# GraphSAGE aggregation on one Trainium2 core: output blocks scaled by GpSimd, gather positions added by GpSimd

## The chip, the cores and the metric

The kernel runs on one core of one Trainium2 chip. The metric is device time in microseconds (us), the median of several runs. The engines go by the names of the profile: PE (TensorE matmul) and PEld (its weight loads), DVE (VectorE), ACT (ScalarE), POOL (GpSimd) and SP (SyncE, which here only issues transfers). Each engine works through its own instructions in order; semaphores tie the engines together. SBUF is the core's working memory, PSUM the memory that PE writes its sums to; ACT and DVE read PSUM here, POOL does not.

## The reference

A graph has N = 12500 nodes with D = 64 features each and E = 800000 edges (source, destination). For each node the features of its neighbours are summed, scaled by the inverse of its degree, and two small matrix products are added.

```python
N, deg, D = 12500, 64, 64
E = N * deg
def reference(x, src, dst, deg_inv, w_self, w_neigh):
    N = x.shape[0]
    nsum = _segment_sum(x[src], dst, N)
    h_neigh = nsum * deg_inv[:, None]
    return x @ w_self + h_neigh @ w_neigh
```

The edges are random, so gathering and scattering 800000 rows is the work. `deg_inv` is a factor per destination node; since it scales whole rows, it can be applied before or after the product with `w_neigh`.

## The kernel before, in words

The kernel first sorts and then multiplies. Each edge becomes one 32-bit key made of a destination block (82 x 2 nodes), a source block (128 nodes) and the two places within them. In the first half DVE sorts 128 runs of 6250 keys (`sort_runs`), cuts them at super-rows, gathers the pieces by indirect transfers, and merges them (`merge_runs`). There are three parts, part 0, 1 and 2, with 29, 20 and 10 buckets a row; a bucket is one pair of destination block and source block. Meanwhile `self_terms` writes `x @ w_self` to the output.

In the second half `nodes` walks over 7546 buckets, eight at a time; eight buckets are a tile, and one iteration of the loop is one tile. For each set of 28 buckets DVE builds two sets of one-hot matrices: `ohs` (L935), from the source places that SP has loaded to `slb` (L933), and `ohd` (L940), from the destination places. PE multiplies `ohs` with the table of features into the PSUM tile `ct` (L966); ACT evicts `ct` to `xg` (L976), and late in the kernel DVE does some of these evictions (L974); PE multiplies `xg` with `ohd` into two accumulators `acc` (L1047). Keys that fit in no bucket are fetched one by one by POOL's indirect transfers into `lx` (L997) and added by one more pair of matmuls (L1015).

After six destination blocks (588 buckets, some 74 tiles) the accumulators are copied to `g`, and `finish` makes two output blocks of 4 x 123 nodes from it: PE multiplies with the weights into the PSUM tile `po` (L1114), ACT evicts it to the SBUF tile `o` and scales each of the four sub-blocks by its own column of `self.deg` (L1117), and, five tiles of the loop later, POOL issues the transfer that adds `o` to the output in memory (L1123). There are 26 such blocks; the last has one sub-block of 123 nodes and one of 77. `po` takes one of the three PSUM buffers that `ct` uses.

While part 0 is being multiplied, parts 1 and 2 are still merged by DVE, a little per tile (`PACE`). When a part is merged, `change` finds its buckets: for bucket column k DVE counts how many keys of each row lie below (L708, into column k of `acc`), four columns later ACT adds the base position and writes an unsigned integer (L762, into `ix`), and POOL gathers the window of 128 rows at those positions into `v` (L742). `decode_buckets` then splits the keys (DVE, L782), narrows them (ACT, L791 to L796) and lets POOL store them to `sl` (L794), from which `slb` is loaded. The narrowed tiles `l16` have two buffers, so ACT waits for the stores. Part 1 has 20 columns and part 2 has 10; part 0 goes another way, with DVE doing the positions.

The order on each engine is that of the Python code (`manual_schedule`): `finish`, `change` and the gathers of `lx` are placed by counts of tiles, not by due times. So POOL's queue in the second half holds, in one order, the gathers of `lx` and `v`, the stores of `sl` and of merged rows, and the output's transfers.

Of the kernel before, what the change touches and what calls it, by code (L numbers as in the profile page):

```python
# [17 lines left out]
OP = mybir.AluOpType  # L18
AF = mybir.ActivationFunctionType
# [3 lines left out]
N, E, D = 12500, 800000, 64  # L23
# [350 lines left out]
class Kernel:  # L374
# [371 lines left out]
    def find_and_gather(self, part, vp):  # L746


        nc = self.nc
        kpr = KPRS[part]  # L750
        self.v = vp.tile([128, kpr, 2 * SIDE], I32, name="v")
        acc = self.keep.tile([128, kpr], F32, name=f"acc2_{part}")
        ix = self.keep.tile([128, kpr], U32, name=f"ix2_{part}")
        junk = vp.tile([128, max(n for _, n in WIN.w2[part])], BF, name="junk")
        for k in range(kpr + LAG):
            if k == 1:
                self.store_rows(part, nc.gpsimd)
            if k < kpr:
                self.count_below(part, k, acc, junk)
            if k >= LAG:  # L760
                g = k - LAG
                nc.scalar.activation(ix[:, g:g + 1], acc[:, g:g + 1], AF.Relu, bias=self.c2[part][:, 3, g:g + 1])  # L762
                self.gather_window(part, g, ix)
            yield k

# [339 lines left out]
    def finish(self, qq, g, pool, mps, w, add=False):  # L1105

        nc = self.nc
        if not add:
            own = self.load_own(qq, pool)
        po = mps.tile([FB, 4, D], F32, name="po", tag="ct", bufs=3)  # L1110
        o = pool.tile([FB, 4, D], F32, name="o", bufs=2)
        for b0, nb, n, r in self.sets(qq):
            for b in range(b0, b0 + nb):
                nc.tensor.matmul(po[:n, b], g[:, b * FB:b * FB + n], w[:g.shape[0]], start=True, stop=True)  # L1114
        for b0, nb, n, r in self.sets(qq):
            for b in range(b0, b0 + nb):
                nc.scalar.activation(o[:n, b], po[:n, b], AF.Copy, scale=self.deg[:n, 4 * qq + b:4 * qq + b + 1])  # L1117
        yield
        for b0, nb, n, r in self.sets(qq):
            at = slice(b0, b0 + nb)  # L1120
            out = self.O["out"][r:r + nb * n].rearrange("(b p) f -> p b f", p=n)
            if add:
                nc.gpsimd.dma_start(out, o[:n, at], accum_op=OP.add)  # L1123
            else:
                nc.vector.tensor_tensor(o[:n, at], o[:n, at], own[:n, at], op=OP.add)
                nc.gpsimd.dma_start(out, o[:n, at])
# [286 lines left out]
```

## Time and profile before

| what | value |
|---|---|
| median of 3 runs | 1871.68 us (1863.13 to 1876.03) |
| profiled execution, own time | 1856.37 us |
| its span, first to last instruction | 1854.6 us |
| mean granted clock of PE | 0.775 |
| DVE busy in the span | 1718.2 us (93%) |
| ACT busy in the span | 1116.7 us (60%) |
| PE busy in the span | 986.6 us (53%) |
| POOL busy in the span | 576.2 us (31%) |
| ACT evicting `xg` (L976) | 919 operations, 862.6 us |
| ACT evicting `o` (L1117) | 102 operations, 24.3 us |
| ACT adding positions (L762) | 30 operations, 10.2 us |

A row of a group of instructions reads: line, engine, operation, the tile written <- the tiles read, shape written <- shape read, xcount, then busy us and mean ns of one, then the idle time of the engine just before them and what ended it. A row of the timeline has start, duration (both us), engine, line, operation, and in brackets the idle time before it and its releaser. A row of waits has who waited for whom, then us in total, times, longest us. Busy time is the union of an engine's instructions; neighbours on ACT overlap a little, so a row's mean can be longer than its distance to the next start.

### The profile page before, as it was taken

How to read it: one execution, taken by the hardware profiler on the slowest of the kernel's cores; microseconds unless marked ns; L12 is line 12 of the kernel's file. 1: busy time of each engine (PE TensorE's matmuls, PEld its weight loads, DVE VectorE, ACT ScalarE, POOL GpSimd, SP SyncE). 2: the span in 40 equal slices, each digit the busy share in tenths (PEclk: the TensorE clock that was granted, in tenths of full speed). 3: DMA queues.
4: the chain of work that ended last, by engine and by line, in shares of the span. 5: the costliest groups of instructions: out<-in, count | busy, mean ns of one | idle time of the engine just before them, and what ended most of it. 6: DMA issues, size and time to landing. Idle time of an engine off the chain costs nothing.

```text
span 1854.6 us, 54153 instructions
## 1 busy us (share of the span) xinstructions
PE 986.6 (53%) x23413; PEld 851.9 (46%) x23413; DVE 1718.2 (93%) x1718; ACT 1116.7 (60%) x1587; POOL 576.2 (31%) x447
## 2 busy tenths in 40 slices
PE   3046000000000000058979979897898899888996
PEld 1015000000000000057868868776887788777885
DVE  6999999999999999989989999998898799978885
ACT  5263000113001005458979989899999899977885
POOL 2000000055502005404456535473332523532331
PEclk7567555555555555579989999999999999999998
DMA  5207100021002002169978888996889788977894
GB/s 174 54 0 169 39 0 0 38 79 51 18 4 73 10 0 82 47 216 266 274 249 253 251 248 254 296 282 227 264 250 284 234 265 242 326 200 257 274 268 118
DMA packets 176789, 307.79 MB, mean 166 GB/s; under 512 B 127885, under 2 KB 133596, under 8 KB 175772
## 3 DMA queue, kind: packets, MB, share of 16 engines
q1 hardware_dynamic: 98268, 275.58, 44.9%
q0 software_dynamic: 78272, 28.65, 9.6%
q8 instruction: 185, 3.03, 0.7%
q14 instruction: 64, 0.52, 0.1%
HBM read 277.01 MB, written 26.52 MB: 164 GB/s over the span
## 4 chain that ended last, share of the span: by engine, by line
DVE 19%; PE 13%; DMA 11%; issue 10%; SPq 5%; POOL 4%; ACT 4%; DVEq 0%; POOLq 0%; ACTq 0%
DMA slb<-sl 10%; PE ct L966 7%; DVE u L328 7%; PE acc L1047 5%; SPq L933 5%; DVE ohs L935 4%; DVE ohd L940 3%; ACT xg L976 2%; DVE u L362 2%; POOL u L565 1%; POOL lx L997 1%; POOL out L1123 1%; DVE u L316 1%; DMA sl<-l 1%; PE acc L1015 1%
## 5 line engine op out<-in xcount | busy, mean ns | idle before, releaser
L976 ACT ACTIVATE xg<-ct 128x1024 f16<-128x1024 f32 x919 | 862.6, 1074 | 104.4 <-PE ct L966 80.0
L966 PE MATMUL ct<-xh,ohs 128*128 128x128 f16 x7546 | 532.6, 224 | 87.9 <-DVE ohs L935 23.7
L966 PEld LDWEIGHTS <-ohs 128*128 128x128 f16 x7546 | 451.8, 100 | 125.4 <-issue 52.5
L328 DVE TENSOR_TENSOR u<-u 128x1512 f32<-128x1512 f32 (+57 forms) x316 | 425.7, 1362 | 12.9 <-ACT u L312 8.6
L1047 PE MATMUL acc<-ohd,xg 64*128 64x82 f16 x15092 | 395.2, 201 | 47.7 <-ACT xg L976 20.4
L1047 PEld LDWEIGHTS <-xg 64*128 64x128 f16 x15092 | 324.6, 96 | 104.6 <-issue 29.2
L997 POOL DMA_INDIRECT lx<-xt,ls x127 | 232.0, 1826 | 425.6 <-PE acc L1015 352.5
L940 DVE TENSOR_TENSOR ohd<-iota,dlT 128x2296 f16<-128x2296 bf16 x270 | 362.2, 1341 | 0.0
L935 DVE TENSOR_SCALAR ohs<-slb,pidx 128x3584 f16<-128x3584 bf16 x270 | 321.8, 1192 | 40.2 <-DMA slb<-sl 19.0
L509 PE MATMUL stp<-cx,swapa 128*128 128x16 f32 (+1 forms) x12 | 3.1, 335 | 398.0 <-DVE swapa L505 398.0
L260 DVE TENSOR_TENSOR a<-b 128x1040 f32<-128x1040 f32 (+41 forms) x130 | 194.7, 1539 | 3.5 <-DVE b L260 0.5
L260 DVE TENSOR_TENSOR b<-a 128x1040 f32<-128x1040 f32 (+46 forms) x150 | 194.6, 1345 | 3.2 <-ACT a L262 0.4
L538 POOL DMA_INDIRECT u<-d,ixa x48 | 72.5, 1511 | 390.8 <-ACT junka L526 335.4
L509 PEld LDWEIGHTS stp<-cx,swapa 128*128 128x128 f32 x12 | 2.6, 271 | 398.5 <-DVE swapa L505 398.5
L312 ACT ACTIVATE u<-u 128x256 f32<-128x256 f32 (+14 forms) x60 | 33.0, 618 | 170.6 <-DVE u L316 134.8
L1123 POOL DMA_DIRECT2D out<-o x27 | 99.1, 3800 | 103.1 <-ACT o L1117 89.8
L802 PE MATMUL tr<-idb,l 128*128 128x128 bf16 x59 | 7.6, 263 | 188.9 <-ACT l L796 188.9
L262 ACT ACTIVATE b<-a 128x2 f32<-128x2 f32 (+31 forms) x41 | 15.9, 402 | 127.1 <-DVE a L260 120.4
L802 PEld LDWEIGHTS <-l 128*128 128x128 bf16 x59 | 4.3, 114 | 191.2 <-ACT l L796 190.8
L316 DVE TENSOR_TENSOR u<-u 128x2016 f32<-128x2016 f32 (+11 forms) x40 | 61.9, 1563 | 16.2 <-DMA u<-da,ixb 8.8
L262 ACT ACTIVATE a<-b 128x1 f32<-128x1 f32 (+24 forms) x34 | 8.6, 259 | 105.4 <-DVE b L260 99.9
L565 POOL DMA_INDIRECT u<-da,ixb x24 | 36.9, 1539 | 88.6 <-ACT ixb L513 85.0
(158 smaller groups left out, 839.4 us busy)
## 6 DMA issues: line engine op xcount, KB each, us to landing
slb<-sl SPq DMA_DIRECT2D x1076, 224.0 KB
xt<-xh SPq DMA_DIRECT2D x1, 3136.0 KB
out<-o POOLq DMA_DIRECT2D x25, 123.0 KB
own<-os SPq DMA_DIRECT2D x12, 256.0 KB
out<-os SPq DMA_DIRECT2D x12, 256.0 KB
rd<-dst SPq DMA_DIRECT2D x5, 512.0 KB
rs<-src SPq DMA_DIRECT2D x5, 512.0 KB
lx<-xt,ls POOLq DMA_INDIRECT x127
```

Source lines behind the costliest of these rows:

```text
L260: nc.vector.tensor_tensor(view(dst, lo + sh, [[st, g], [1, l]]), x, y, op=op)
L316: nc.vector.tensor_tensor(at(oth, to, n), x, y, op=op)
L328: nc.vector.tensor_tensor(to, at(cur, ln + lo, n), at(cur, lo + k, n), op=op)
L538: nc.gpsimd.indirect_dma_start(out=u[:, i * w:(i + 1) * w], out_offset=None, in_=src, in_offset=bass.IndirectOffsetOnAxis(ap=self.start[pa ...
L933: nc.sync.dma_start(b[j::4], bass.AP(tensor=src.tensor, offset=src.offset, ap=[[0, 32], [1, n * 128]]))
L935: nc.vector.tensor_scalar(s.rearrange("p c s -> p (c s)"), b, self.pidx[:, :1], None, op0=OP.is_equal)
L940: nc.vector.tensor_tensor(d, self.iota[:, None].to_broadcast(wide), ix, op=OP.is_equal)
L966: nc.tensor.matmul(ct[:, i * 128:(i + 1) * 128], cols[i][0], self.xh[:, (b0 + i) % NB].rearrange("p a f -> p (a f)"), start=True, stop=True)
L976: nc.scalar.activation(xg[:, :cnt * 128], ct[:, :cnt * 128], AF.Copy)
L997: nc.gpsimd.indirect_dma_start(out=x, out_offset=None, in_=self.xt, in_offset=bass.IndirectOffsetOnAxis(ap=self.left[p][1][:, c:c + 1].bit ...
L1047: nc.tensor.matmul(acc[h][:, db % OCT * HN:(db % OCT + 1) * HN], xg[r, i * 128:(i + 1) * 128], d[r], start=db % OCT == 0 and sb == 0, stop ...
L1123: nc.gpsimd.dma_start(out, o[:n, at], accum_op=OP.add)
```

## The change

Two places change. In `finish`, one ACT operation without a factor evicts all sub-blocks of a set from `po` to `o`, and one POOL `tensor_tensor` multiplies `o` in place with the degree factors, each column of `self.deg` broadcast along the 64 features. In the gathers of parts 1 and 2, the addition of the base position moves from ACT (with a Relu) to POOL, on the queue that issues the gather itself.

```diff
@@ -759,7 +759,7 @@
             if k >= LAG:
                 g = k - LAG
-                nc.scalar.activation(ix[:, g:g + 1], acc[:, g:g + 1], AF.Relu, bias=self.c2[part][:, 3, g:g + 1])
+                nc.gpsimd.tensor_scalar(ix[:, g:g + 1], acc[:, g:g + 1], self.c2[part][:, 3, g:g + 1], None, op0=OP.add)
                 self.gather_window(part, g, ix)
             yield k
@@ -1113,8 +1113,10 @@
         for b0, nb, n, r in self.sets(qq):
-            for b in range(b0, b0 + nb):
-                nc.scalar.activation(o[:n, b], po[:n, b], AF.Copy, scale=self.deg[:n, 4 * qq + b:4 * qq + b + 1])
+            at = slice(b0, b0 + nb)
+            nc.scalar.activation(o[:n, at], po[:n, at], AF.Copy)
+            scale = self.deg[:n, 4 * qq + b0:4 * qq + b0 + nb]
+            nc.gpsimd.tensor_tensor(o[:n, at], o[:n, at], scale[:, :, None].to_broadcast([n, nb, D]), op=OP.mult)
         yield
```

## The prediction

> **What bounds the kernel now.** I read the page first. Its busy rows and the strips of 40 slices (46.4 us each) show two halves.
>
> ```profile
> span 1854.6 us, 54153 instructions
> ...
> PE 986.6 (53%) x23413; PEld 851.9 (46%) x23413; DVE 1718.2 (93%) x1718; ACT 1116.7 (60%) x1587; POOL 576.2 (31%) x447
> ...
> DVE  6999999999999999989989999998898799978885
> ACT  5263000113001005458979989899999899977885
> ```
>
> Up to slice 16 (about 790 us) DVE sorts and ACT has little to do; nothing in the change lies there. From slice 18 on, where the sums of the nodes run, DVE and ACT both show 8s and 9s. So I asked for windows of that half (columns: PE, PEld, DVE, ACT, POOL busy, then granted clock, DMA share, GB/s).
>
> ```profile
> 1000.00:1200.00 200.00, 176.20 (x4518) 155.88 (x4513) 197.28 (x203) 181.43 (x218) 94.45 (x40) 0.97 0.87 263
> 1200.00:1300.00 100.00, 86.10 (x2117) 74.41 (x2115) 90.72 (x138) 96.20 (x139) 50.95 (x39) 0.97 0.82 258
> 1300.00:1600.00 300.00, 270.07 (x6851) 239.27 (x6848) 277.69 (x333) 280.78 (x364) 115.47 (x67) 0.97 0.86 262
> ...
> sum 965.00, PE 837.70 PEld 742.75 DVE 873.78 ACT 855.45 POOL 396.04; mean PE 139.62 PEld 123.79 DVE 145.63 ACT 142.57 POOL 66.01
> ```
>
> No single engine bounds this half: DVE leads from 1000 to 1200 us (98.6%), ACT from 1200 to 1300 (96.2%), and the DMA engines stand at 0.82 to 0.87. POOL has room (396 of 965 us). The chain of waits, for 890 to 1845 us, says which of them ends last:
>
> ```profile
> by line: DMA slb<-sl 17.7%; issue 17.3%; PE ct L966 12.0%; PE acc L1047 9.0%; SPq L933 7.6%; DVE ohs L935 7.2%; DVE ohd L940 5.3%; ACT xg L976 4.3%; DVE u L328 3.3%; POOL u L565 2.5%; POOL lx L997 1.7%; POOL out L1123 1.5%; DMA sl<-l 1.0%;
> ```
>
> Two loops carry it. One is DVE (ohs, ohd, u: 15.8%) with the slb loads that a finished ohs sets free (DMA 17.7%, SPq 7.6%): 41.1% together. The other is PE; ACT's evictions are only 4.3%. The table of waits for the same stretch agrees that ACT is as often waiting as waited for:
>
> ```profile
> ACT xg L976 <- PE ct L966: 70.9, 88, 8.0
> ...
> PE ct L966 <- ACT xg L976: 21.1, 23, 3.8
> ...
> PE acc L1047 <- ACT xg L976: 20.4, 15, 4.8
> ```
>
> ACT stood 88 times for PE, once in some 11 us; PE stood 41.5 us for ACT.
>
> **What ACT loses.** The two lines that change, in the groups, and their places in ACT's timeline (start, us, what):
>
> ```profile
> L1117 ACT ACTIVATE o<-po,deg 123x64 f32<-123x64 f32 x102 | 24.3, 351 | 7.5 <-PE po L1114 7.1
> ...
> L762 ACT ACTIVATE ix<-acc,c 128x1 uint32<-128x1 f32 x30 | 10.2, 339 | 0.0
> ...
> 981.01 0.93 ACT L1117 ACTIVATE o<-po,deg 123x64 f32<-123x64 f32 x4
> 981.81 12.93 ACT L976 ACTIVATE xg<-ct 128x1024 f16<-128x1024 f32 x14
> ...
> 1223.72 0.34 ACT L762 ACTIVATE ix<-acc,c 128x1 uint32<-128x1 f32 x1
> 1223.90 1.99 ACT L976 ACTIVATE xg<-ct 128x1024 f16<-128x1024 f32 x2
> ...
> 1836.98 0.38 ACT L976 ACTIVATE xg<-ct 128x256 f16<-128x256 f32 x1 [0.68 <-PE ct L966]
> ```
>
> The mean durations mislead: the next operation starts before the last has ended. From start to start four evictions take 0.80 us and one position 0.18 us. An eviction of 256 columns from PSUM takes 0.38 us by the last row, which I count as 0.28 from start to start (the x4 row overlaps its successor by 0.13 us, so 0.1 is an estimate from it). Of the 102 evictions 100 are 25 whole blocks; the last block keeps its two narrow ones. ACT so loses 25 x (0.80 - 0.28) = 13.0 us and 30 x 0.18 = 5.4 us, 18.4 us in all.
>
> How much of it reaches the end? Bounds: ACT's share of the chain gives 0.043 x 18.4 = 0.8 us, everything gives 18.4. Where ACT leads, 1200 to 1300 us, I count all: by the source lines' own windows there are 14 of the 30 positions and 8 narrow evictions (two blocks) there.
>
> ```profile
> 1200.00:1300.00 100.00, 5.46 (x14) 0.97 0.82 258
> ...
> 1200.00:1300.00 100.00, 2.01 (x8) 0.97 0.82 258
> ```
>
> That is 14 x 0.18 + 2 x 0.52 = 3.6 us. Of the other 14.8 us I count a tenth, 1.5 us, nearer to the chain's 4.3% than to ACT's busy share, since a wait for PE that comes every 11 us swallows a saving of 0.2 to 0.5 us. Term: **-5 us**.
>
> **What POOL gains.** 27 multiplications (25 of 123x256, two of 64 columns) and 30 additions of one column. No row of before has POOL arithmetic on two inputs. The nearest are these:
>
> ```profile
> L396 POOL MEMSET edge<- 128x1 f32 x1 | 0.1, 98 | 0.0
> ...
> masks.py:197 POOL MEMSET idf<- 128x128 f32 x1 | 0.2, 204 | 0.3 <-POOLq L1403 0.3
> ...
> masks.py:199 POOL TENSOR_SCALAR_AFFINE_SELECT idf<-idf 128x128 f32<-128x128 f32 x1 | 0.3, 282 | 0.0
> ...
> masks.py:199 POOL TENSOR_SCALAR_AFFINE_SELECT idb<-idb 128x128 bf16<-128x128 bf16 x1 | 1.2, 1246 | 0.0
> ```
>
> Writing costs 98 ns and 0.83 ns a column; reading one input adds 78 ns over 128 columns, 0.6 ns each. Two inputs over 256 columns: 98 + 256 x (0.83 + 1.2) = 0.62 us, so I take 0.6. The floor is writing alone, 0.31 us; the ceiling is the slow bf16 row taken twice, 2.5 us. An addition I take as 0.2 us (0.1 to 0.3). POOL's own 27 x 0.6 + 30 x 0.2 = 22.2 us fit in its idle time; what counts is whom they hold up.
>
> **DVE** first. POOL and DVE do hold each other up in this trace (a memset of 0.20 us beside the ohs of DVE, then an ohs beside the output's DMA):
>
> ```profile
> 1441.90 0.20 POOL L425 MEMSET pad<- 128x100 f32 x1
> ...
> 1443.87 1.03 POOL L425 MEMSET pad<- 128x100 f32 x1
> ...
> 1443.63 1.16 DVE L935 TENSOR_SCALAR ohs<-slb,pidx 128x3584 f16<-128x3584 bf16 x1 [0.59 <-PE ct L966]
> ...
> 1468.87 4.15 POOL L1123 DMA_DIRECT2D out<-o  x1 [2.87 <-ACT o L1117]
> ...
> 1469.28 2.48 DVE L935 TENSOR_SCALAR ohs<-slb,pidx 128x3584 f16<-128x3584 bf16 x1
> ...
> L940 DVE TENSOR_TENSOR ohd<-iota,dlT 128x2296 f16<-128x2296 bf16 x247 | 331.3, 1341 | 0.0
> L935 DVE TENSOR_SCALAR ohs<-slb,pidx 128x3584 f16<-128x3584 bf16 x246 | 294.1, 1195 | 31.0 <-PE ct L966 18.3 <-DMA slb<-sl 12.0 <-DVE ohd L940 0.2
> L328 DVE TENSOR_TENSOR u<-u 128x736 f32<-128x736 f32 (+43 forms) x160 | 157.5, 995 | 1.8 <-ACT u L312 0.7
> ```
>
> The memset took 1.03 us and ended at 1444.90, just after the ohs (1444.79); the ohs took 2.48 us where its like took 1.16. By what these rows show, ohs is the one that collides: it fills 294.1 of 955 us, 31%, so DVE would lose 0.31 x 22.2 = 6.9 us. The bounds are nothing (POOL always waits) and all of DVE's lines with two inputs besides (331.3 + 294.1 + 157.5 = 782.9 us, 82%): 18.2 us. I weigh it with the 41.1% of DVE's loop in the chain: 2.8 us, nearest to the ohs row, the only one that stretched. Term: **+3 us**.
>
> The Trainium skill (SBUF — State Buffer, "Who interferes with whom") has a rule against this change: DVE and GpSimd share one pair of ports as an exclusive lock, held for the whole instruction, and a DVE instruction with two SBUF inputs collides with a GpSimd one that reads SBUF. For ohs the trace agrees (2.48 against 1.16 us); for the two-input lines no run here shows it, since POOL's rows beside them only write or issue. By that rule the loss would be the 82% bound, 18.2 us, and the term +7.5 in place of +3.
>
> **POOL's queue** next. An addition takes the place of a wait for ACT, but it waits for DVE; a multiplication stands five tiles ahead of its output's DMA and waits for ACT, and the lx, v and sl transfers behind it wait too. Elsewhere POOL idles between two lx; the one full stretch is this (POOL, then ACT):
>
> ```profile
> 1224.33 1.38 POOL L742 DMA_INDIRECT v<-d,ix  x1 [3.82 <-ACT ix L762]
> ...
> 1249.78 1.70 POOL L997 DMA_INDIRECT lx<-xt,ls  x1 [0.30 <-issue]
> 1252.60 0.58 POOL L794 DMA_DIRECT2D sl<-l  x1 [1.12 <-ACT l L792]
> ...
> 1257.99 0.72 ACT L791 ACTIVATE l<-w,edge 128x512 bf16<-128x512 int32 x1 [1.03 <-DMA sl<-l]
> ...
> 1208.16 0.07 DVE L708 DVE_READ_ACCUMULATOR junk<-u,c 128x1 f32 x1
> ```
>
> The gather at 1224.33 (first row) is the thirteenth of part 1; its count was ready on DVE at 1208.2 (last row), so the 3.82 us of waiting for ACT fall away. Behind it stand 8 additions at 0.2 + 0.3 (the gap before a gather) and 2 multiplications at 0.6 + 0.3: 5.8 us. Later by 2.0 us, of which the idle 1.12 before the sl store covers most: **+0.9 us** on ACT, which waits for that store. If each of the ten also waits out a DVE operation, as the memset did (0.83 us), it is +9. If the cover went altogether, the l16 buffers would halt ACT, and PE after it.
>
> **The tail** has nothing beside it:
>
> ```profile
> 1840.68 1.31 ACT L1117 ACTIVATE o<-po,deg 123x64 f32<-123x64 f32 x6 [1.34 <-PE po L1114]
> ...
> 1842.04 5.22 POOL L1123 DMA_DIRECT2D out<-o  x3 [38.41 <-ACT o L1117]
> ```
>
> ACT ends 0.5 us sooner; POOL adds one wide multiplication (0.6) and two narrow (0.2 to 0.3 each): **+0.7 us** (0 to 1.5). PE gets its po buffer back 0.5 us sooner, 25 times; that is inside ACT's term. Order of work on PE, DVE and SP stays.
>
> **Sum.** -5 + 3 + 0.9 + 0.7 = -0.4, about nothing. The profiled execution took 1856.37 us (span 1854.6), 0.8% below the median of 1871.68, so I add the difference to the median: 1871 us.
>
> **The rivals.** *ACT's saving comes through whole.* For it: ACT is over 90% busy in each window from 1000 to 1600 us, and PE stood 41.5 us for it. Against: the 70.9 us it stands for PE. -18.4 + 0.9 + 0.7 = -17: 1855 us. Chance 0.2.
>
> *POOL's multiplications shut DVE out.* The mechanism is the collision above on all two-input lines, from 890 us on, at DVE's busy share of 0.905 (873.78 of 965) instead of 0.41. For a multiplication of p us DVE loses 0.82 x (27p + 6), and 0.905 of it lengthens the kernel; with -3.4 for the other terms p = 0.6 gives +13, p = 1.25 (the slow row once) +26, p = 2.5 +51. It passes 1% (18.7 us) from p = 0.88. For it: DVE's 98.6%, the slow row of 1.25 us. Against: the f32 row of 0.28. Time at p = 1.25: 1898 us, slower. Chance 0.2, of which 0.13 over 1%. The rule of the Trainium skill above is what would make this one true.
>
> *POOL's queue at 1224 to 1253 us becomes the bound*, ten operations each behind one of DVE: +9 in place of +0.9, 1879 us. For it: no idle time there. Against: positions no longer wait for ACT. Chance 0.07. That four evictions don't become one cheaper one is excluded by the 0.38 us row.
>
> **The numbers.** The forecast has 0.53. 1% is about what a measurement of this kernel can tell from no change. Faster by over 1% needs more than the whole of ACT's relief, by gathers that start earlier: 0.08. Slower: 0.13 from DVE and 0.02 from the queue: 0.15. The rest, 0.77, is within 1%. The range goes from the first rival, 1855, to most of the second, 1893; within it the likeliest case alone has 1863 to 1880.
>
> **What the changed profile would show.** ACT's busy sum falls by 15 to 25 us; one eviction of 123x256 near 0.38 us; no L762 on ACT. POOL's multiplication: 0.6 us when alone (the last one, at the tail), more beside DVE. Under my DVE term L940 keeps its 1341 ns and L935's mean rises by some 25 ns; under the rule L940's mean and maximum rise too. The sl store near 1252 us no more than 2 us late against its neighbours. I am wrong if POOL's arithmetic takes over 1 us alone, or if DVE's two-input lines stretch by over 15 us in sum.

## The result and the profile after

The changed kernel took 1880.87 us (median of 20 runs, 1875.99 to 1888.2), the kernel before in the same comparison 1870.25 us (20 runs, 1859.97 to 1882.86). The ratio is 1.0058 with a 95% interval of 1.004 to 1.0076: slower by some 11 us. That is inside the forecast range (1855 to 1893 us) and within 1%, but the forecast was no change, and the interval excludes that. The profiled execution took 1880.58 us. The one of before was a quick one of its kernel (1856.37 us), so the 24 us between the two profiles overstate the 11 us between the medians; sizes below come from ratios, places from profiles.

The page of the changed kernel, the lines that answer to those of before:

```profile
span 1878.9 us, 54114 instructions
...
PE 989.1 (53%) x23413; PEld 853.4 (45%) x23413; DVE 1727.4 (92%) x1718; ACT 1104.1 (59%) x1482; POOL 651.8 (35%) x504
...
DVE  6999999999999999989989999987998799988986
ACT  5263000122001006279979989969899898977885
```

ACT is relieved by 12.6 us (1116.7 to 1104.1), where the forecast had 15 to 25. DVE's sum grew by 9.2 us. POOL's grew by 75.6 us, where the forecast had 22.2. In the strips ACT falls to 6 in the 27th slice, 1221 to 1268 us, and DVE to 8 and 7 in that and the next; before, ACT had a 9 there and DVE a 9 and an 8. The windows of the changed kernel (PE, PEld, DVE, ACT, POOL busy, granted clock, DMA share, GB/s) show the same place:

```profile
1000.00:1200.00 200.00, 176.47 (x4575) 155.61 (x4570) 197.61 (x201) 181.43 (x203) 113.17 (x47) 0.98 0.88 264
1200.00:1300.00 100.00, 72.97 (x1752) 63.26 (x1745) 78.44 (x113) 79.10 (x103) 70.40 (x52) 0.88 0.76 228
1300.00:1600.00 300.00, 269.87 (x6760) 238.73 (x6760) 275.00 (x338) 273.64 (x329) 120.33 (x73) 0.95 0.85 256
```

From 1200 to 1300 us PE did 72.97 us of work instead of 86.10, ACT 79.10 instead of 96.20, DVE 78.44 instead of 90.72: all three stood still for some 12 to 17 us, and only POOL did more (70.40 instead of 50.95). The granted clock was lower there too, 0.88 instead of 0.97. The windows before and behind it are nearly those of before. The waits of the changed kernel from 1220 to 1310 us name the chain (who waited for whom: us in total, times, longest):

```profile
PE acc L1047 <- ACT xg L976: 19.7, 4, 15.7
...
DVE w L782 <- ACT l L792: 16.9, 2, 14.4
ACT l L791 <- DMA sl<-l: 15.2, 1, 15.2
```

PE and DVE wait for ACT, and ACT for a transfer of `sl`. In POOL's and ACT's timeline of the changed kernel (start, duration, what, idle before):

```profile
1232.93 1.86 POOL L742 DMA_INDIRECT v<-d,ix  x1 [0.27 <-POOL ix L762]
...
1261.61 3.60 POOL L1125 DMA_DIRECT2D out<-o  x1
1263.61 1.97 POOL L762 TENSOR_SCALAR ix<-acc,c 128x1 uint32<-128x1 f32 x1
1265.86 1.10 POOL L742 DMA_INDIRECT v<-d,ix  x1 [0.28 <-POOL ix L762]
1267.26 0.98 POOL L997 DMA_INDIRECT lx<-xt,ls  x1 [0.30 <-issue]
1268.20 0.65 POOL L794 DMA_DIRECT2D sl<-l  x1
...
1272.21 0.72 ACT L791 ACTIVATE l<-w,edge 128x512 bf16<-128x512 int32 x1 [15.22 <-DMA sl<-l]
```

The `sl` store that ACT needs to get its `l16` buffer back was issued at 1252.60 us before, with 1.12 us of idle POOL ahead of it. Now it is issued at 1268.20 with none, and ACT stands 15.22 us. The first row, the thirteenth gather of part 1, was at 1224.33 before. So of the 15.6 us that the store is late, 8.6 were lost ahead of that gather, with the twelve gathers in front of it, and 7.0 behind it; the first gather of part 1 is at 1182.20 in place of 1182.72, so nothing was lost earlier. The groups of the changed kernel show what filled POOL's queue and what became of the two DVE lines of the prediction:

```profile
L940 DVE TENSOR_TENSOR ohd<-iota,dlT 128x2296 f16<-128x2296 bf16 x270 | 364.9, 1351 | 0.0
L935 DVE TENSOR_SCALAR ohs<-slb,pidx 128x3584 f16<-128x3584 bf16 x270 | 323.7, 1199 | 50.6 <-PE ct L966 24.1 <-DMA slb<-sl 18.5 <-issue 5.1
L762 POOL TENSOR_SCALAR ix<-acc,c 128x1 uint32<-128x1 f32 x30 | 41.6, 1387 | 2.6 <-DVE junk L708 1.7
L1119 POOL TENSOR_TENSOR o<-o,deg 123x256 f32<-123x256 f32 (+2 forms) x27 | 30.6, 1194 | 90.0 <-ACT o L1117 89.9
L1117 ACT ACTIVATE o<-po 123x256 f32<-123x256 f32 (+2 forms) x27 | 10.5, 394 | 8.4 <-PE po L1114 4.3 <-issue 3.6
```

An addition to one column takes 1387 ns on average, not 200; a multiplication 1194, not 600. What an addition takes depends on what DVE does beside it, as POOL's and DVE's timelines of the changed kernel show, the additions first:

```profile
1183.26 2.20 POOL L762 TENSOR_SCALAR ix<-acc,c 128x1 uint32<-128x1 f32 x1
...
1186.79 0.31 POOL L762 TENSOR_SCALAR ix<-acc,c 128x1 uint32<-128x1 f32 x1
...
1182.84 1.30 DVE L935 TENSOR_SCALAR ohs<-slb,pidx 128x3584 f16<-128x3584 bf16 x1 [0.53 <-PE ct L966]
1184.06 1.33 DVE L940 TENSOR_TENSOR ohd<-iota,dlT 128x2296 f16<-128x2296 bf16 x1
...
998.05 0.76 POOL L1119 TENSOR_TENSOR o<-o,deg 123x256 f32<-123x256 f32 x1 [2.31 <-ACT o L1117]
...
998.26 1.77 DVE L940 TENSOR_TENSOR ohd<-iota,dlT 128x2296 f16<-128x2296 bf16 x1
```

The first addition began during `ohs`, lasted through it and through the whole `ohd` behind it, and ended at 1185.46, just after `ohd` (1185.39). The second began at 1186.79, behind DVE's last operation of that moment, and took 0.31 us. DVE isn't the whole of it: two of the 30 additions, the longest (4.05 us) and the one at 1263.61, began while POOL itself was still issuing the transfer of `out`. The latter had no DVE operation beside it; it ended at 1265.58, just behind that issue (1265.21). The last two rows show the other direction: a multiplication that began before `ohd` made that `ohd` take 1.77 us instead of 1.34.

### The profile page after: what moved, and what is told of

It reads as the page before. It is cut to its first block, busy times and chain, and to the rows that moved or that the text cites. A ratio compares the mean times of both kernels' runs of the same rounds, so it can differ in the third digit from the quotient of the medians.

```text
span 1878.9 us, 54114 instructions
## 1 busy us (share of the span) xinstructions
PE 989.1 (53%) x23413; PEld 853.4 (45%) x23413; DVE 1727.4 (92%) x1718; ACT 1104.1 (59%) x1482; POOL 651.8 (35%) x504
## 4 chain that ended last, share of the span: by engine, by line
DVE 19%; PE 14%; DMA 12%; issue 8%; SPq 6%; ACT 4%; POOL 4%; DVEq 0%; POOLq 0%; ACTq 0%
DMA slb<-sl 11%; PE ct L966 7%; DVE u L328 7%; SPq L933 6%; PE acc L1047 5%; DVE ohs L935 4%; DVE ohd L940 3%; ACT xg L976 2%; DVE u L362 2%; POOL lx L997 1%; POOL u L565 1%; POOL out L1125 1%; DVE u L316 1%; DMA sl<-l 0%; PE acc L1015 0%
## 5 line engine op out<-in xcount | busy, mean ns | idle before, releaser
L328 DVE TENSOR_TENSOR u<-u 128x1512 f32<-128x1512 f32 (+57 forms) x316 | 426.6, 1365 | 12.9 <-ACT u L312 7.9
L1047 PE MATMUL acc<-ohd,xg 64*128 64x82 f16 x15092 | 399.5, 202 | 68.2 <-ACT xg L976 27.5
L997 POOL DMA_INDIRECT lx<-xt,ls x127 | 247.3, 1947 | 397.9 <-PE acc L1015 307.7
L1125 POOL DMA_DIRECT2D out<-o x27 | 99.3, 3690 | 10.2 <-POOL o L1119 5.4
L316 DVE TENSOR_TENSOR u<-u 128x2016 f32<-128x2016 f32 (+11 forms) x40 | 62.0, 1564 | 10.2 <-DMA u<-da,ixb 9.8
```

The lines of the kernel that those rows point to most:

```text
L316: nc.vector.tensor_tensor(at(oth, to, n), x, y, op=op)
L328: nc.vector.tensor_tensor(to, at(cur, ln + lo, n), at(cur, lo + k, n), op=op)
L997: nc.gpsimd.indirect_dma_start(out=x, out_offset=None, in_=self.xt, in_offset=bass.IndirectOffsetOnAxis(ap=self.left[p][1][:, c:c + 1].bit ...
L1047: nc.tensor.matmul(acc[h][:, db % OCT * HN:(db % OCT + 1) * HN], xg[r, i * 128:(i + 1) * 128], d[r], start=db % OCT == 0 and sb == 0, stop ...
```

## The experiments

Each is compared with the kernel before on the same chip, five rounds each. The first four ran together (before: 1859.41 us), then the next four (1859.70), the next four (1859.91) and the last three (1867.80). 0.1% is 1.9 us.

**Each part alone.** First the positions on POOL, with the blocks as before:

```diff
-nc.scalar.activation(ix[:, g:g + 1], acc[:, g:g + 1], AF.Relu, bias=self.c2[part][:, 3, g:g + 1])
+nc.gpsimd.tensor_scalar(ix[:, g:g + 1], acc[:, g:g + 1], self.c2[part][:, 3, g:g + 1], None, op0=OP.add)
```

> The positions alone move to POOL; the blocks are evicted and scaled by ACT as before. Two theories. Queue theory: the 30 one-column additions take 1.4 us each because they wait out DVE's two-input operations, POOL's queue is late, the sl stores behind it are late and ACT stands at its two l16 buffers; then this part alone carries the whole loss: +10 to +18 us (ratio 1.005 to 1.010), and ACT's L791 stands 10 us or more for the sl store. DVE theory: the loss is DVE time that POOL's wide multiplications take; then this kernel is as fast as before or faster by ACT's 5 us (ratio 0.997 to 1.001), though its additions are as long.

Measured: ratio 1.0055 (1.0038 to 1.0071), that is +10.2 us. The waits of this kernel from 1220 to 1310 us hold the same stop, and its window the same loss on PE:

```profile
ACT l L791 <- DMA sl<-l: 16.3, 1, 16.3
...
1200.00:1300.00 100.00, 74.61 (x1821) 65.41 (x1819) 78.69 (x115) 82.62 (x113) 66.76 (x49) 0.90 0.74 222
```

Then the blocks alone, with the positions on ACT as before (one eviction, one multiplication by POOL):

```diff
-nc.gpsimd.tensor_scalar(ix[:, g:g + 1], acc[:, g:g + 1], self.c2[part][:, 3, g:g + 1], None, op0=OP.add)
+nc.scalar.activation(ix[:, g:g + 1], acc[:, g:g + 1], AF.Relu, bias=self.c2[part][:, 3, g:g + 1])
```

> The blocks alone change (one eviction by ACT, scaling by POOL); the positions stay on ACT. Queue theory: -6 to +2 us (ratio 0.997 to 1.001), since POOL has room wherever the multiplications stand and ACT loses 13 us; L791 stands about 1 us for the sl store. DVE theory: the multiplications cost DVE some 0.4 us each, 27 times, on its loop: +8 to +11 us (ratio 1.004 to 1.006).

Measured: 1.0028 (1.0008 to 1.0049), +5.2 us. Its window shows no such stop; ACT's longest wait for the `sl` store is 5.7 us here, against 5.4 in the kernel without scaling below, which lost nothing:

```profile
1200.00:1300.00 100.00, 83.79 (x2032) 72.94 (x2032) 89.11 (x125) 92.03 (x129) 59.27 (x41) 0.93 0.81 245
```

So both parts cost, in different ways. The long stop belongs to the positions alone.

**More buffers where ACT stopped.** The changed kernel with four `l16` buffers in parts 1 and 2 instead of two, at both places where they are made:

```diff
-l16 = vp.tile([128, 4, 128], BF, name="l16", bufs=2 if part else 4)
+l16 = vp.tile([128, 4, 128], BF, name="l16", bufs=4)
```

> The changed kernel with four l16 buffers instead of two for parts 1 and 2, so that ACT can narrow two groups ahead of the stores. Queue theory in its narrow form: the stop is ACT at l16; L791's 15.8 us for the sl store fall below 3 us and the time falls to that of before or below (ratio 0.996 to 1.002). If the late gathers themselves are what stops the rest (DVE waiting for v), or by the DVE theory, the ratio stays at 1.004 to 1.008.

Measured: 1.0043 (1.0024 to 1.0063). This interval overlaps with that of the change, and the wait is only shorter by 2.3 us:

```profile
ACT l L791 <- DMA sl<-l: 12.9, 1, 12.9
```

Two more buffers don't outlast the delay. The run therefore doesn't decide whether the buffers or the gathers behind them set the stop.

**No addition on POOL.** The changed kernel, with the positions added by DVE, four columns at a time:

```diff
-nc.gpsimd.tensor_scalar(ix[:, g:g + 1], acc[:, g:g + 1], self.c2[part][:, 3, g:g + 1], None, op0=OP.add)
+if g % 4 == 0:
+    e = min(g + 4, kpr)
+    nc.vector.tensor_tensor(ix[:, g:e], acc[:, g:e], self.c2[part][:, 3, g:e], op=OP.add)
```

> The changed kernel with the positions added on DVE, four columns by one tensor_tensor (8 operations in place of 30), so that neither ACT nor POOL adds them; blocks as in the changed kernel. Queue theory: POOL's queue is as short as before, ACT has lost 18 us, DVE gained 8 x 0.2 us: ratio 0.995 to 1.000. DVE theory: the multiplications are still there: ratio 1.004 to 1.006.

Measured: 1.0050 (1.0032 to 1.0069). The long stop is gone, as the window shows (ACT's longest wait for the store is 1.9 us), but the time stays above the 0.995 to 1.000 expected from the queue alone. The loss that stays is that of the blocks, whose interval alone (1.0008 to 1.0049) this one meets. By this run alone the gain over the change's first measurement (1.0058) isn't clear of noise.

```profile
1200.00:1300.00 100.00, 84.61 (x2080) 73.54 (x2074) 94.02 (x149) 92.42 (x118) 54.30 (x41) 0.97 0.84 258
```

**What ACT's relief is worth.** One eviction for four, and no multiplication anywhere: the degree factor is left out of the neighbours' term.

```diff
-            for b in range(b0, b0 + nb):
-                nc.scalar.activation(o[:n, b], po[:n, b], AF.Copy, scale=self.deg[:n, 4 * qq + b:4 * qq + b + 1])
+            at = slice(b0, b0 + nb)
+            nc.scalar.activation(o[:n, at], po[:n, at], AF.Copy)
```

> One eviction by ACT instead of four, and no scaling at all (the factor of the degree is left out, so the rows are not the reference's); positions on ACT as before. It takes POOL's multiplications out of the blocks-alone kernel, which took 1.0028 (1.0008 to 1.0049). If the multiplications cost what that kernel lost (DVE held by POOL, 8 us of DVE time), this one is faster than the blocks-alone kernel by 0.3% or more: ratio 0.995 to 0.999. If the loss has nothing to do with POOL's arithmetic (the single eviction itself, or chance in how the engines fall together), the ratio stays at 1.002 to 1.005.

Measured: 0.9998 (0.9983 to 1.0013), between -3.2 and +2.4 us. The 13 us that ACT no longer spends on blocks buy nothing that can be measured.

**The store taken out of POOL's queue.** Positions on POOL, blocks as before, and the `sl` stores of parts 1 and 2 issued by ACT:

```diff
-nc.scalar.activation(ix[:, g:g + 1], acc[:, g:g + 1], AF.Relu, bias=self.c2[part][:, 3, g:g + 1])
+nc.gpsimd.tensor_scalar(ix[:, g:g + 1], acc[:, g:g + 1], self.c2[part][:, 3, g:g + 1], None, op0=OP.add)
...
-(nc.gpsimd if part else nc.sync).dma_start(rows[:, k:k + n], l16[:, :n])
+(nc.scalar if part else nc.sync).dma_start(rows[:, k:k + n], l16[:, :n])
```

> The positions-alone kernel (1.0055) with the sl stores of parts 1 and 2 issued from ACT's queue instead of POOL's. Queue theory: the gathers are as late as in that kernel, but the stores no longer stand behind them, ACT does not stand 16 us at l16, and most of the 10 us come back: ratio 0.997 to 1.002. If the late gathers themselves are the stop (DVE's splitting waits for v instead), DVE's w stands 8 us or more for the v transfer and the ratio stays at 1.004 to 1.007.

Measured: 1.0029 (1.0009 to 1.0048), between the two expectations, where the positions alone had 1.0055; the intervals overlap a little. ACT's stop has gone from 16.3 to 0.2 us. What is late next is the gather itself, once, on DVE; and the issue takes time on ACT (rows of this kernel, waits from 1220 to 1310 us, then ACT's timeline):

```profile
DVE w L782 <- DMA v<-d,ix: 9.9, 1, 9.9
ACT l L791 <- DMA sl<-l: 0.2, 1, 0.2
...
1256.78 0.33 ACTq L794 DMA_DIRECT2D sl<-l  x1
1257.30 0.63 ACT L796 ACTIVATE l<-v 128x512 bf16<-128x512 int32 x1 [0.56 <-DVE ohd L940]
```

So the late store is what stops ACT, and POOL's gathers are late besides.

**Before, with the positions on DVE.** The same four-column addition by DVE in the kernel before, blocks untouched, in two separate comparisons:

```diff
-nc.scalar.activation(ix[:, g:g + 1], acc[:, g:g + 1], AF.Relu, bias=self.c2[part][:, 3, g:g + 1])
+if g % 4 == 0:
+    e = min(g + 4, kpr)
+    nc.vector.tensor_tensor(ix[:, g:e], acc[:, g:e], self.c2[part][:, 3, g:e], op=OP.add)
```

> Only the positions change: DVE adds them, four columns by one tensor_tensor (8 operations in place of ACT's 30); blocks as before. ACT loses 5.4 us, DVE gains 8 x 0.2 = 1.6 us, POOL's queue has no addition and no wait for ACT. Queue theory: ratio 0.996 to 1.000, and the sl store is not late. If merely taking the additions from ACT's place in the order disturbs the rest, 1.003 to 1.006 as for the positions-alone kernel.

> The kernel with the positions added by DVE in eights of an operation's cost (8 operations for 30 columns), blocks as before, measured a second time, since its first interval (0.9962 to 1.0003) just holds 1. ACT has lost 5.4 us, which the kernel without scaling showed to be worth little, and POOL no longer waits for ACT at the positions: ratio 0.997 to 1.000.

Measured: 0.9983 (0.9962 to 1.0003) and 1.0001 (0.9983 to 1.0019). Taking 5.4 us from ACT, and giving DVE 1.2 us for it, changes nothing that can be measured. The same additions on POOL cost 10.2 us (1.0038 to 1.0071), so it is their place on POOL that costs:

```profile
L764 DVE TENSOR_TENSOR ix<-acc,c 128x4 uint32<-128x4 f32 (+1 forms) x8 | 1.2, 152 | 0.0
```

**A POOL operation that only writes.** The kernel before, with one more POOL operation in the queue ahead of each of the 30 gathers, one column wide, that reads nothing:

```diff
 nc.scalar.activation(ix[:, g:g + 1], acc[:, g:g + 1], AF.Relu, bias=self.c2[part][:, 3, g:g + 1])
+nc.gpsimd.memset(self.pad[:, :1], 0.0)
```

> The kernel before with one more POOL instruction ahead of each of the 30 gathers: a one-column memset, which writes and does not read SBUF; positions stay on ACT. Same number of POOL instructions as the positions-alone kernel. If it is reading beside DVE that makes the addition long, the memset is held by ohs alone, takes 0.1 us in most cases and 0.3 to 0.5 us in the mean against 1.39 us, and the ratio is 1.000 to 1.003. If any POOL instruction there is as costly, its mean is over 1 us and the ratio 1.004 to 1.007.

Measured: 1.0018 (0.9996 to 1.004). The source lines' own view (minimum, median, maximum in ns), first this kernel's memset, then the changed kernel's addition at the same place:

```profile
L763 POOL MEMSET pad<- x30: 112/118/2505, 1174.6 to 1596.6; 128x1 f32 x30
```

```profile
L762 POOL TENSOR_SCALAR ix<-acc,c x30: 303/1380/4053, 1179.0 to 1623.0; 128x1 uint32<-128x1 f32 x30
```

Written only, a column is mostly done in 118 ns beside the same DVE; read and written, half of them take more than 1380 ns. So the operation's work isn't what makes it long. Waiting is, and beside DVE the wait falls on the operation that reads. The two memsets of over 2 us (2.48 and 2.50) began while POOL was still issuing `out`, as two of the additions did; the longer one in POOL's timeline of this kernel:

```profile
1236.20 4.20 POOL L1124 DMA_DIRECT2D out<-o  x1
1238.13 2.50 POOL L763 MEMSET pad<- 128x1 f32 x1
```

In time the two kernels are less clearly apart: the upper end of this interval (1.004) just passes the lower end of that of the positions alone (1.0038).

**Is it the place of the multiplication in POOL's queue?** Blocks alone, with the multiplication moved from behind the eviction to just ahead of the output's transfer, five tiles of the loop later:

```diff
             nc.scalar.activation(o[:n, at], po[:n, at], AF.Copy)
-            scale = self.deg[:n, 4 * qq + b0:4 * qq + b0 + nb]
-            nc.gpsimd.tensor_tensor(o[:n, at], o[:n, at], scale[:, :, None].to_broadcast([n, nb, D]), op=OP.mult)
         yield
...
             at = slice(b0, b0 + nb)
+            scale = self.deg[:n, 4 * qq + b0:4 * qq + b0 + nb]
+            nc.gpsimd.tensor_tensor(o[:n, at], o[:n, at], scale[:, :, None].to_broadcast([n, nb, D]), op=OP.mult)
```

> The blocks-alone kernel (1.0028) with POOL's multiplication moved to just ahead of the block's output DMA, five tiles later, where ACT has long evicted the block: the multiplications are the same, but POOL's queue does not wait for ACT at them ahead of the lx gathers. If they cost by holding DVE (read beside read), nothing changes: ratio 1.002 to 1.005, DVE's excess as in blocks-alone. If they cost by the wait they bring into POOL's queue, it falls to that of the kernel without scaling: 0.998 to 1.001.

Measured: 1.0048 (1.003 to 1.0067), no less than with the multiplication at its first place (1.0028). But the edit took little of the wait away. POOL's waits over the whole span, first of this kernel, then of the kernel before:

```profile
POOL o L1122 <- ACT o L1117: 81.6, 14, 36.8
```

```profile
POOL out L1123 <- ACT o L1117: 89.8, 14, 38.4
```

Blocks alone have 92.4 us of it. So POOL stood for ACT's evictions as long before the change, there at the transfer itself: the wait isn't what the multiplications add. Nor is the `sl` store the price here: the waits of this kernel show none of ACT for it.

**The multiplication twice.** Blocks alone, with a second, equal multiplication behind the first, so that the neighbours' term is scaled twice:

```diff
 nc.gpsimd.tensor_tensor(o[:n, at], o[:n, at], scale[:, :, None].to_broadcast([n, nb, D]), op=OP.mult)
+nc.gpsimd.tensor_tensor(o[:n, at], o[:n, at], scale[:, :, None].to_broadcast([n, nb, D]), op=OP.mult)
```

> The blocks-alone kernel with each multiplication made twice (the rows so get the factor twice and are not the reference's). If the 27 multiplications cost what stands between the kernel without scaling (0.9998) and blocks-alone (1.0028), 0.3%, by DVE's time, 27 more cost as much again: ratio 1.004 to 1.008, DVE's busy sum another 5 to 9 us up. If the cost is the wait for ACT in POOL's queue or chance, a second one behind the first adds 0.001 at most: 1.002 to 1.004.

Measured: 1.0072 (1.0038 to 1.0106), +13.4 us, some two and a half times the cost of one multiplication, with a wide interval. DVE's whole busy sum hardly moved (1725.9 us with one, 1727.2 with two, where 5 to 9 us more were expected), because `ohs` had less (319.8 us in place of 326.4). The lines that stretch are `ohd` and `ohl`, first with one multiplication, then with two:

```profile
L940 DVE TENSOR_TENSOR ohd<-iota,dlT 128x2296 f16<-128x2296 bf16 x270 | 364.0, 1348 | 0.0
...
L1006 DVE TENSOR_SCALAR ohl<-wide,lp 128x164 f16<-128x164 f16 (+1 forms) x127 | 40.5, 325 | 0.0
```

```profile
L940 DVE TENSOR_TENSOR ohd<-iota,dlT 128x2296 f16<-128x2296 bf16 x270 | 367.0, 1359 | 0.0
...
L1006 DVE TENSOR_SCALAR ohl<-wide,lp 128x164 f16<-128x164 f16 (+1 forms) x127 | 44.3, 355 | 0.0
```

In all kernels of this document the mean of `ohd` is 1348 to 1359 ns where POOL multiplies, and 1341 to 1345 where it doesn't. The mean of `ohs` shows no such order.

**The changed kernel again**, beside the three runs that stand with it:

> The changed kernel itself, on the chip of these runs, for the sum of its parts: positions alone took 1.0055 and blocks alone 1.0028. If the parts add up it is 1.007 to 1.010; the first measurement said 1.0058 (1.004 to 1.0076). If they share a wait (the positions' late sl store gives ACT a rest in which the blocks' cost is hidden), 1.005 to 1.007.

Measured: 1.0094 (1.007 to 1.0118). The parts alone add up to 1.0055 + 0.0028 = 1.0083, between this and the 1.0058 of the result. So they add, as far as intervals of this width can say.

**Is it POOL's reading?** Blocks alone, with the multiplication replaced by two memsets of `o`, which write as much and read nothing; the neighbours' term is left out of the output:

```diff
-nc.gpsimd.tensor_tensor(o[:n, at], o[:n, at], scale[:, :, None].to_broadcast([n, nb, D]), op=OP.mult)
+for _ in range(2):
+    nc.gpsimd.memset(o[:n, at], 0.0)
```

> Blocks-alone with each of POOL's multiplications replaced by two memsets of the same 256 columns, which wait for ACT and hold up the output's DMA as the multiplication does and take as long alone (two of about 0.3 us), but read nothing; the neighbours' term is so left out of the output. If the multiplications cost by reading beside DVE's two-input lines, the cost goes: ratio 0.999 to 1.0015, DVE's ohd keeps 1342 ns, a memset about 0.4 us in the mean. If it is POOL's time and its place in the queue, whatever it does there, the ratio stays at 1.003 to 1.005, like blocks-alone (1.0028 and, multiplied later, 1.0048).

Measured: 1.0031 (1.0005 to 1.0057). The groups and the source line of this kernel:

```profile
L940 DVE TENSOR_TENSOR ohd<-iota,dlT 128x2296 f16<-128x2296 bf16 x270 | 362.7, 1343 | 0.0
L935 DVE TENSOR_SCALAR ohs<-slb,pidx 128x3584 f16<-128x3584 bf16 x270 | 331.2, 1227 | 66.5 <-PE ct L966 37.5 <-DMA slb<-sl 24.1 <-PE acc L1047 2.9
...
L1119 POOL MEMSET o<- x54: 142/311/1730, 894.9 to 1873.0; 123x256 f32 x50, 123x64 f32 x2, 77x64 f32 x2
```

Writing alone leaves `ohd` at 1343 ns. The mean of `ohs` is 1227 (1196 in the kernel without any scaling), but by starts and ends in the trace only 6 of the 270 `ohs` ran beside a memset of POOL, five of them with nothing else of POOL beside them and at 1.21 us on average. The excess lies in 31 `ohs` beside POOL's issue of a plain transfer, with 1.78 us on average where the kernel before has 35 with 1.47. In time the memsets may cost as much as the multiplication. That reading is what the blocks pay for isn't supported.

**The multiplication on DVE** instead of POOL, otherwise as in blocks alone:

```diff
-nc.gpsimd.tensor_tensor(o[:n, at], o[:n, at], scale[:, :, None].to_broadcast([n, nb, D]), op=OP.mult)
+nc.vector.tensor_tensor(o[:n, at], o[:n, at], scale[:, :, None].to_broadcast([n, nb, D]), op=OP.mult)
```

> Blocks-alone with the multiplication made by DVE instead of POOL: a known amount of DVE time, 25 x 0.4 = 10 us, and no POOL arithmetic. It says what a microsecond of DVE in the second half is worth, which the prediction put at 0.41: at that weight +4 us (ratio 1.002); at the busy share of 0.9 it is +9 us (1.005). If POOL's multiplications cost by the 5 to 9 us of DVE time that they add, this one must cost at least as much as they do, 1.003 to 1.006; if DVE's time is worth little here, 1.000 to 1.002, and their cost lies elsewhere.

Measured: 1.0050 (1.0024 to 1.0076). Its source line says how much DVE time was added:

```profile
L1119 DVE TENSOR_TENSOR o<-o,deg x27: 215/420/428, 893.7 to 1852.5; 123x256 f32<-123x256 f32 x25, 123x64 f32<-123x64 f32 x1, 77x64 f32<-77x64 f32 x1
```

25 x 0.42 and two short ones are about 11 us on DVE, and the kernel became longer by 9.3 us (4.5 to 14.2), with ACT's relief, worth nothing, in it. Put down to the work alone, a microsecond of DVE is worth some 0.85, by the interval 0.4 to 1.3. That is an upper reading: DVE also stood 15.4 us ahead of these multiplications, 11.4 of them for ACT's eviction, and the run doesn't say which part of that it would have stood anyway.

**A version that might beat both:** the kernel before, with positions on DVE in fours and the `sl` stores issued by ACT.

```diff
-nc.scalar.activation(ix[:, g:g + 1], acc[:, g:g + 1], AF.Relu, bias=self.c2[part][:, 3, g:g + 1])
+if g % 4 == 0:
+    e = min(g + 4, kpr)
+    nc.vector.tensor_tensor(ix[:, g:e], acc[:, g:e], self.c2[part][:, 3, g:e], op=OP.add)
...
-(nc.gpsimd if part else nc.sync).dma_start(rows[:, k:k + n], l16[:, :n])
+(nc.scalar if part else nc.sync).dma_start(rows[:, k:k + n], l16[:, :n])
```

> Blocks as before, positions added by DVE (8 operations), and the sl stores of parts 1 and 2 issued by ACT. POOL's queue then holds neither additions nor stores, ACT loses 5.4 us and does not wait for POOL at l16. Queue theory: ratio 0.995 to 1.000, L791 stands under 1 us for the sl store.

Measured: 1.0049 (1.0028 to 1.007), not the 0.995 to 1.000 expected, though ACT no longer stands for the `sl` store. In ACT's timeline of this kernel the groups of four gathered columns start 6.69 us apart (1262.26, 1268.95, 1275.64), where before they came after 1257.99 and 1263.98, 6.0 us:

```profile
1262.26 0.75 ACT L793 ACTIVATE l<-w,edge 128x512 bf16<-128x512 int32 x1
...
1263.80 0.33 ACTq L796 DMA_DIRECT2D sl<-l  x1
1264.32 0.63 ACT L798 ACTIVATE l<-v 128x512 bf16<-128x512 int32 x1 [0.56 <-ACT l L794]
...
1268.95 0.75 ACT L793 ACTIVATE l<-w,edge 128x512 bf16<-128x512 int32 x1
```

The issue opens a gap of 0.56 us between two operations that otherwise overlap. Eight stores at some 0.7 us are 5 to 6 us of ACT's time, but 13 us less of it were worth nothing above, so that doesn't explain the loss. The window says where it is, not why:

```profile
1200.00:1300.00 100.00, 83.29 (x1885) 71.43 (x1884) 83.50 (x122) 86.34 (x116) 43.72 (x33) 0.90 0.76 228
```

PE did 1885 matmuls there in place of 2117, while ACT was busy for 86.34 us in place of 96.20, so more work on ACT isn't what held them up. No version tried beats the kernel before by more than the noise.

## Why the prediction was wrong

The total was 11 us (0.6%) too low, and three of the four terms were too low: measured one by one, ACT's relief is worth 0 in place of -5, the blocks' load on DVE +5.2 in place of +3, and the positions on POOL +10.2 in place of +0.9. These add up to 15.4 us, more than the 10.6 of the medians and less than the 17.6 of the repetition. The forecast took 1% for what a measurement can tell from no change; twenty runs of each kernel told 0.6%, with an interval of 0.2% to either side.

- **POOL's queue, +0.9 us: the step that failed.** The step priced an addition at 0.2 us and charged no wait for DVE. It is 0.30 alone and 1.39 on average. The step also counted only what stands behind the thirteenth gather, as if the queue reached it on time; the twelve gathers ahead of it, with their additions, made it 8.6 us late, more than the 3.82 us of waiting for ACT that fell away. The cover I named, 1.12 us of idle POOL ahead of the `sl` store, was gone, and what I wrote would follow then did: the `l16` buffers halted ACT, and PE after it. The part costs 10.2 us (7.1 to 13.2). The third rival had this mechanism at +9, with 0.83 us of waiting for each operation; it was given 0.07 because positions no longer wait for ACT. That advantage was real and small. The price leaned on rows of memsets, which only write, and the memset experiment shows that such rows don't stand for an operation that reads. The store, forecast no more than 2 us late, was 15.6 us late. The 15 us of the stop are more than the 10 us at the end. The kernel without scaling had 5.4 us of this wait and lost nothing, so not every microsecond of it counts; what gives the rest back wasn't isolated.
- **ACT, -5 us: nothing.** The price of an eviction was right (394 ns for 0.38 us forecast); ACT's sum fell by 12.6 us, under the 15 to 25 forecast. What that is worth was wrong: the kernel without scaling says 0 (-3.2 to +2.4) for 13 of the 18.4 us, and positions on DVE say the same for the other 5.4. The chain's share of ACT, 4.3%, would have given 0.8 us; counting all of the saving from 1200 to 1300 us, because ACT is 96% busy there, was the error. The rival of a whole gain, 1855 us, is excluded.
- **DVE, +3 us: near in size, wrong in the line, the weight open.** The loss of 6.9 us was near: DVE's sum is 9.2 us above before in the changed kernel, and 4.2 above the kernel without scaling where only blocks change (1725.9 against 1721.7). The blocks alone cost +5.2 us (1.5 to 9.1). The weight of 0.41, DVE's share of the chain, is at the lower end of what the multiplication on DVE allows (0.4 to 1.3, with its 0.85 an upper reading), so it is neither shown nor excluded. The line was wrong: `ohs` was to stretch by 25 ns and `ohd` not at all; measured are 7 and 10. The `ohs` of 2.48 us that the step rested on stood beside the issue of `out`, not beside arithmetic; in the kernel before, 35 `ohs` beside an issue of a plain transfer took 1.47 us on average, those with nothing of POOL beside them 1.14.
- **The rule and the second rival.** That every line of DVE with two inputs gives way was priced at 18.2 us on DVE. The trace agrees in kind (the `ohd` of 1.77 us beside a multiplication) and not in size: beside 27 multiplications of 1.19 us on average `ohd` grew by 2.7 us in sum and `u` (L328) by 0.9. With the 0.61 us that a multiplication takes alone the second rival gives +13 us, near the 10.6 measured, but by luck: most of the loss came from the positions, and DVE's two-input lines didn't stretch by that much. For the same reason neither sign of being wrong came (arithmetic of over 1 us alone, 15 us more on the two-input lines), and yet the forecast was wrong: no sign watched the additions' wait. The Trainium skill (SBUF — State Buffer, "Who interferes with whom") says that whoever issues first holds the pair for the whole instruction and the other blocks. The rows of the additions agree that POOL blocks, and go further: the addition at 1183.26 let not one but two DVE operations go ahead of it. So POOL paid for most of the collision, with two thirds of its time in these lines (72.2 us where 30 x 0.30 + 25 x 0.61 are 24.3; the waits behind an issue of `out` are in it), and DVE little. The same section of the Trainium skill also says that a DVE operation with two inputs collides with a POOL operation that reads and not with one that only writes; the memsets agree (118 ns at the median, `ohd` at 1343 ns in the kernel with memsets of `o`).
- **The tail, +0.7 us: too small to matter.** From ACT's last evictions to the end of the span were 13.9 us before (1854.6 - 1840.68) and 14.0 after (1878.9 - 1864.91). The wide multiplication, with nothing of DVE beside it, takes 0.61 us, the forecast price:

```profile
1864.91 0.68 ACT L1117 ACTIVATE o<-po 123x256 f32<-123x256 f32 x3 [1.39 <-PE po L1114]
...
1865.38 0.61 POOL L1119 TENSOR_TENSOR o<-o,deg 123x256 f32<-123x256 f32 x1 [35.43 <-ACT o L1117]
```

Open are three things. The first is by which path the blocks cost 5 us, and why two multiplications cost twice the time of one while DVE's whole sum stays; the delay may lie in DVE's order beside PE rather than in its sum, and no run shows it. The second is whether the two memsets cost by the same path as the multiplication, since their interval reaches from almost nothing to more than the multiplication's. The third is what slowed the last version.

## What to carry to other kernels

Price an operation that moves to POOL by what runs beside it, not by its own work: a POOL operation that reads waited out one or two DVE operations here, and in a queue that also issues gathers and stores this wait is paid by whoever waits for those. Add it up from the first such operation in the queue, not from the stretch that looks full. Before moving work off an engine, find what that engine's time is worth by leaving the work out: here 13 us less on an ACT that was over 90% busy were worth nothing, while 11 us of work put on DVE, with the waits that came with it, made the kernel 9.3 us longer. Where the cover of a term is a single microsecond of idle time, give the case without it more than a small chance.

## What was not expected of the hardware

- The smallest POOL operation with an input took 0.30 us alone and 1.38 us at the median, beside DVE operations of up to 1.35 us each; a memset of the same column took 0.118 us at the median. The worst of both (4.05 and 2.50 us) began while POOL was still issuing the transfer of `out`.
- Memsets of `o` by POOL left `ohd`, with its two inputs, at 1343 ns; the multiplications brought its mean to between 1348 and 1359. In the kernel before, `ohs`, with one input, took 1.47 us on average beside POOL's issue of a plain transfer and 1.14 with nothing of POOL beside it.
- Issuing a transfer from ACT's queue took a record of 0.33 us and a gap of 0.56 us between ACT's operations; groups of four columns were 6.69 us apart with it and 6.0 without.
